# Other slots for the weight-combination steps, other places for three loads, and another order in the last batch, in a fused attention and two-layer MoE kernel

## The chip, the cores and the metric

One core of a Trainium2 chip runs the whole program in one launch. The metric is device time in microseconds (us). Engines are called as in the profile: PE (matmul), PEld (its weight loads), DVE (vector), ACT (scalar), POOL (GpSimd) and SP, the engine whose queue issues nearly every DMA here.

## What is computed

```python
# per batch of 8, per head: q, k, v are 576 x 64, p is 32 x 64
p_packed = softmax(scale * p @ k.T) @ v
x = softmax(scale * q @ p_packed.T) @ p_packed      # heads side by side: 4608 tokens x 512
h = x @ w_in;   g = h * cos(h);                 y = g @ w_out      # first MoE, 512 -> 2048 -> 512
h = y @ w_in2;  g = where(h >= 1, h, where(h <= -1, 0, (h + 1)**2 / 4));  out = g @ w_out2
```

## The kernel before

Activations are kept transposed, features on the partitions and tokens along the row. A batch is 576 tokens, two halves of 288 (`HB`), so nearly every elementwise instruction handles 128 x 576 elements and every large matmul has 288 columns. An fp32 product is made of three fp32r matmuls (`TERMS`): each operand is split into a high part (a rounding copy on ACT) and a low part (the difference, on DVE or POOL), and high x high, high x low and low x high are added up.

The program has four stages. Stage 1 does attention and the first up product (`up`, L503). Stage 2, `run_down1`, does the first down product with the cosine. Stages 3 and 4, `run_up2` and `run_down2`, are the second MoE, and the change lies in them. There the 2 x 2 block product is done with seven products instead of eight; they are called X1, Z6, Y5, X2, Z7, Y3 and Z4. The first letter names the accumulator in PSUM (`psX`, `psY`, `psZ`; two banks of Z, one of X and of Y): X1, Y5 and Z6 start it, the others are added to what stands there. So between two products on one accumulator somebody has to read the first result out: X1 is copied to `p1` by ACT, Z6 + p1 becomes `u` on DVE, Y5 + p1 becomes `q` on DVE; the sums `hh` are the four block results.

The seven products need combined inputs and combined weights.

- Combined weights (`su` of the up product, `sd` of the down product) are made by `combine` (L425), a generator with 13 steps for one unit of 2 x 128 rows: two loads; a scaling on ACT (L137); five conversion steps on DVE over 128 x 1024 elements (L144, L146, L150, L152, L156; the weights arrive as 64-bit numbers); two steps of small sums (L454, L455, L457, L458); then the highs on ACT (L444), the lows on DVE (L447) and the stores. Of the 16 units the last six, all of `sd`, are left for stage 3; the others are done before.
- Combined inputs of the up product come from `make_y` (L546): one load of a batch's y (1152 KB, `yb<-yT`), then eleven steps. Seven make a tile `ty` (the high on ACT, L75, the low on POOL, L76), four are differences on POOL (L558). In stage 3 this is all that POOL does.
- Combined inputs of the down product come from `source` (L849) on DVE and ACT, out of tiles `g` that `load_g` (L845) loads: four quarters b of four tiles each per batch.

Stage 3 runs over 8 batches p, 4 groups f of each and 7 products k of a group in the order X1, Z4 (of the group before), Z6, Y5, X2, Z7, Y3. One product is 12 matmuls, and what is written behind it is called a slot here; a batch has 28 slots, number 28p + 7f/2 + k. Behind product k comes `beside(k)` (L616): DVE sums (L597), the piecewise activation as two ACT instructions (L621, L625) and one on DVE (L629, "select"), and a store of the result `gT`. Nothing reorders this: the text of the program is the order on every engine, since `in_order` chains each engine's instructions as they are written. Two tables place the other work. A slot takes one step of `combine` if its number within the batch is in `UNIT_AT`, from slot `UNIT_FROM` on. `Y_AT` says how many steps of `make_y` for the next batch follow slot (f, k); two more steps follow slots (0, 0) and (0, 2) of the next batch. In the last batch a table `D2_AT` places the first loads of stage 4.

```python
    UNIT_AT = (20, 25, 27, 0, 1, 3, 6, 7, 8, 10, 13, 14, 15)
    Y_AT = {(2, 2): 3, (2, 6): 2, (6, 2): 1, (6, 4): 2, (6, 6): 1}
    ...
    D2_AT[0, 2] = d2_g0
    D2_AT[4, 3] = d2_g1
```

So one unit stretches from slot 20 of a batch to slot 15 of the next, and its heavy DVE steps stand at slots 27, 0, 1, 3 and 6.

Stage 4 goes through (batch, product, quarter c of the depth), each step 12 matmuls, 48 for a product, in the order `ORDER_DN`; the Z4 of a batch comes after X1 of the next one, only the last batch has it at the very end, straight after Z7. In the first steps g = 0, 1, 2, ... the loads stand by hand: at g = 1 quarter 2 of g, at g = 2 the weights of Z6 (2 x 1 MB), at g = 3 quarter 3. SP issues in this order, and its queue lands in this order.

Of the kernel before, what the change touches and what calls it, by code (L numbers as in the profile page):

```python
# [14 lines left out]
ALU = mybir.AluOpType  # L15
# [4 lines left out]
WO_FROM = 36  # L20
N_FIRST = 2
UNITS_1 = 8
UNIT_FROM = 20
FIRST_AT = (0, 5, 10, 13, 14)
SU_AT = tuple(range(70, 94, 4)) + (122, 124, 126, 127)
Y_LOAD = 112
# [3 lines left out]
PI = 3.141592653589793  # L30
TERMS = ((0, 0), (0, 1), (1, 0))
ORDER_UP = ("X1", "Z6", "Y5", "X2", "Z7", "Y3", "Z4")
ORDER_DN = ("X1", "Y5", "X2", "Z6", "Y3", "Z7", "Z4")


@with_exitstack
def body(ctx: ExitStack, tc: tile.TileContext, q, k, v, p, w_in, w_out, w_in2, w_out2, out):
    nc = tc.nc
    B, HP, _, S = q.shape
# [4 lines left out]
    HB = S // 2  # L44
# [46 lines left out]
    def begin_stores(keep=0):  # L91
        while len(stores) > keep:
            dst, src = stores.popleft()
            nc.sync.dma_start(out=dst, in_=src)
# [429 lines left out]
    SW, TY = {}, {}  # L524
# [62 lines left out]
    def wtile(pool, tag, bufs):  # L587
        return pool.tile([128, 2, HB], F32, tag=tag, name=tag, bufs=bufs)
# [197 lines left out]
        up2["rest"] = ys, eng, order[n_su[0]:]  # L786
        pd.close()

    UNIT_AT = (20, 25, 27, 0, 1, 3, 6, 7, 8, 10, 13, 14, 15)
    Y_AT = {(2, 2): 3, (2, 6): 2, (6, 2): 1, (6, 4): 2, (6, 6): 1}  # L790

    def run_up2():
        up2[5] = ctx.enter_context(tc.tile_pool(name="up_5", bufs=1, reuse_waits="tile", side="right"))
        for i in (8, 7, 6):
            up2[i] = pu.enter_context(tc.tile_pool(name=f"up_{i}", bufs=1, reuse_waits="tile", side="right"))
        up2["o"] = ctx.enter_context(tc.tile_pool(name="up_o", bufs=1, reuse_waits="tile"))
        ys, eng, rest = up2.pop("rest")
        old, n_fill = None, [0]
        eng[0] = nc.gpsimd
        for p in range(B):  # L800
            for f in range(0, 8, 2):
                at = {}
                cur = {"at": (p, f)}

                def fill(k):
                    x = 28 * p + f // 2 * 7 + k
                    if x >= UNIT_FROM and x % 28 in UNIT_AT:
                        step("wt")
                    if p == B - 1 and f == 6 and n_r[0] < 4 and k in (1, 3, 5, 6):
                        ahead()  # L810

                for k, o in enumerate(("X1", "Z4", "Z6", "Y5", "X2", "Z7", "Y3")):
                    if k != 1:
                        products_up(p, f, o, cur)
                    elif old:
                        products_up(*old["at"], o, old)
                    if p == f == 0 and k < 4:
                        if rest:
                            load_su(*rest.pop(0)), load_su(*rest.pop(0))
                        if k < 2:  # L820
                            next(ys, None)
                            next(ys, None)
                    beside(k, cur, old, fill)
                    begin_stores(1)
                    if (f, k) in ((0, 0), (0, 2)) and p:
                        next(ys, None)
                    if p + 1 < B:
                        if (f, k) == (0, 3):
                            ys = make_y(p + 1, eng)
                            next(ys)  # L830
                        for _ in range(Y_AT.get((f, k), 0)):
                            next(ys)
                    elif (f, k) in D2_AT:
                        D2_AT[f, k]()
                old = cur
        return old
# [8 lines left out]
    def load_g(p, b, c):  # L845
        t = GB[p, b, c] = GR[(4 * p + b) % 5][c]
        nc.sync.dma_start(out=t, in_=gT[b // 2 * 4 + c, :, 2 * p + b % 2])
# [31 lines left out]
    R = {}  # L879
    d2_seq = []  # L880
    for p_ in range(B):
        for o_ in ORDER_DN[:6]:
            d2_seq.append((p_, o_))
            if o_ == "X1" and p_:
                d2_seq.append((p_ - 1, "Z4"))
# [17 lines left out]
            load_g(0, 1, c)  # L903

    D2_AT[0, 2] = d2_g0
    D2_AT[4, 3] = d2_g1
    D2_AT[4, 0] = lambda: load_sd("X1")
    D2_AT[4, 2] = lambda: load_sd("Y5")
    D2_AT[4, 4] = lambda: load_sd("X2")
# [1 line left out]
    def run_down2(old):  # L911
# [26 lines left out]
        for g, (p, o, c) in enumerate(d2_seq):  # L938
# [3 lines left out]
            x, first = o[0], o in ("X1", "Y5", "Z6")  # L942
            if first and c == 0:
                s[x] = bank(x)
            ps, r = s[x], R.pop((p, o, c))
            for k in range(2):
                f = 2 * c + k
                w_ = SW[o, f // 4]
                for j in range(2):
                    for n, (w, y) in enumerate(TERMS):  # L950
                        nc.tensor.matmul(  # L951
                            out=ps[:, j], lhsT=w_[:, f % 4, w, j * 128:j * 128 + 128], rhs=r[:, y, k],
                            start=first and f == n == 0, stop=f == 7 and n == 2, skip_group_check=True,
                        )
            if g == 0:
                beside(0, None, old, none)
                products_up(*old["at"], "Z4", old)
# [6 lines left out]
            elif g < 5:  # L964
                beside(g + 1, None, old, none)
            begin_stores()
            if g in (1, 3):
                for i in range(4):
                    load_g(0, (g + 3) // 2, i)
            elif g == 2:  # L970
                load_sd("Z6")
            elif g in (5, 9, 12):
                load_sd(ORDER_DN[{5: 4, 9: 5, 12: 6}[g]])
# [2 lines left out]
                    source(*d2_todo.popleft())  # L976
            else:
                finish_source()
        finish(*d2_seq[-1][:2])
        begin_stores()  # L980

    E = mybir.EngineType
    items = [(n, hf, fp) for n, c in FIRST for hf in range(2) for fp in (2 * c, 2 * c + 1)]
# [278 lines left out]
```

## Time and profile before

| what | us |
|---|---|
| median of 3 runs | 1506.61 (1501.76 to 1513.17) |
| the profiled execution's own time | 1511.39 |
| its span on the chip | 1509.6 |
| PE busy in the span | 1470.4 |

Times of rows count from the start of the span. Stage 3 runs from 774.07 to 1142, stage 4 from 1142 to the end. "idle" and the brackets [us <-releaser] tell how long an engine stood idle before an instruction and what ended that.

### The profile page before, as it was taken

The page shows a single profiled execution, that of the slowest core. Times are in us where ns is not written, and L with a number is a line of the kernel's source. Part 1 is how long each engine was busy: PE and PEld are TensorE (multiplying, and loading weights), DVE is VectorE, ACT ScalarE, POOL GpSimd, SP SyncE. Part 2 cuts the span into 40 slices and gives each one's busy share as a digit, 9 for nine tenths or more (in the row PEclk, how much of TensorE's full clock was granted, in tenths as well). Part 3 has the DMA queues.
Part 4 walks back from the last instruction along what each step waited for, and adds up shares of the span by engine and source line. Part 5 has one row for each costly group of instructions (what it writes and reads, how often), then busy time and mean ns, then how long its engine had stood idle before and what let it go on. Part 6 is the DMA issues. An engine that isn't in the chain of part 4 may idle for free.

```text
span 1509.6 us, 29648 instructions
## 1 busy us (share of the span) xinstructions
PE 1470.4 (97%) x11796; PEld 1400.0 (93%) x11796; DVE 1173.9 (78%) x1682; ACT 907.8 (60%) x1424; POOL 139.8 (9%) x85
## 2 busy tenths in 40 slices
PE   8899999998999999999999999999999999999998
PEld 5678777788999999999999999999999999999998
DVE  7784676776888888888856889888867777777876
ACT  4455566667676667666647777777765444444442
POOL 0000000000000000000005335445310000000000
PEclk9899999999999999999999999999999999999999
DMA  9676777577555655766573664564568744344350
GB/s 352 204 236 226 254 272 270 199 238 254 166 162 171 197 186 187 270 219 187 177 286 133 213 210 162 176 218 172 190 240 339 267 153 128 114 134 142 119 157 33
DMA packets 156043, 302.36 MB, mean 200 GB/s; under 512 B 13568, under 2 KB 59648, under 8 KB 152320
## 3 DMA queue, kind: packets, MB, share of 16 engines
q1 hardware_dynamic: 155904, 300.47, 59.1%
q8 instruction: 92, 1.51, 0.4%
q14 instruction: 47, 0.39, 0.1%
HBM read 176.69 MB, written 123.73 MB: 199 GB/s over the span
## 4 chain that ended last, share of the span: by engine, by line
PE 82%; DVE 7%; DMA 7%; issue 2%; ACT 2%; SPq 0%; DVEq 0%; ACTq 0%
PE psZ L747 14%; PE psZ L951 10%; PE hps L512 9%; PE psZ L609 8%; PE psX L747 7%; PE psY L747 7%; PE psY L951 6%; PE psX L951 6%; PE psY L609 5%; PE psX L609 5%; DMA h1T<-u 3%; PE psS L275 2%; PE psM L218 2%; DVE t L629 1%; DMA yb<-yT 1%
## 5 line engine op out<-in xcount | busy, mean ns | idle before, releaser
L512 PEld LDWEIGHTS hps<-at,m 128*128 128x128 f32 x1536 | 209.4, 190 | 49.1 <-ACT u L518 19.9
L512 PE MATMUL hps<-at,m 128*128 128x288 f32 x1536 | 227.2, 303 | 10.4 <-ACT u L518 4.3
L747 PE MATMUL psZ<-r,wo 128*128 128x288 f32 x1536 | 206.1, 295 | 0.0
L747 PEld LDWEIGHTS psZ<-r,wo 128*128 128x128 f32 x1536 | 205.2, 188 | 0.0
L76 POOL TENSOR_TENSOR ty<-yb,ty 128x576 fp32r<-128x576 f32 x51 | 91.0, 1790 | 960.9 <-ACT ty L75 960.5
L857 ACT ACTIVATE r<-g 128x576 fp32r<-128x576 f32 x147 | 96.8, 681 | 125.5 <-DVE g L854 116.8
L715 ACT ACTIVATE r<-t 128x576 fp32r<-128x576 f32 x128 | 87.7, 685 | 129.0 <-PE psY L747 62.1
L720 DVE TENSOR_TENSOR r<-t,r 128x576 fp32r<-128x576 f32 x128 | 97.0, 757 | 57.8 <-ACT r L715 57.6
L518 ACT ACTIVATE u<-hps 128x576 f32<-128x576 f32 x128 | 83.0, 650 | 95.3 <-PE hps L512 58.1
L621 ACT ACTIVATE t<-hh,half 128x576 f32<-128x576 f32 x128 | 98.9, 772 | 50.9 <-DVE hh L597 45.1
L747 PE MATMUL psX<-r,wo 128*128 128x288 f32 x768 | 123.3, 296 | 1.7 <-ACT u L518 1.7
L747 PE MATMUL psY<-r,wo 128*128 128x288 f32 x768 | 123.2, 296 | 0.0
L629 DVE SCALAR_TENSOR_TENSOR t<-hh,t 128x576 f32<-128x576 f32 x128 | 114.0, 910 | 4.8 <-ACT t L625 4.8
L867 DVE TENSOR_TENSOR r<-g,r 128x576 fp32r<-128x576 f32 x147 | 107.4, 752 | 7.1 <-ACT r L857 7.1
L747 PEld LDWEIGHTS psX<-r,wo 128*128 128x128 f32 x768 | 109.4, 188 | 1.9 <-ACT u L518 1.9
L747 PEld LDWEIGHTS psY<-r,wo 128*128 128x128 f32 x768 | 109.4, 188 | 0.0
L951 PE MATMUL psZ<-r,so 128*128 128x288 f32 x768 | 104.6, 295 | 0.9 <-DVE hh L597 0.9
L951 PE MATMUL psY<-r,sw 128*128 128x288 f32 x768 | 104.9, 295 | 0.0
L951 PEld LDWEIGHTS psZ<-r,so 128*128 128x128 f32 x768 | 102.8, 188 | 1.1 <-ACT r L857 1.1
L951 PEld LDWEIGHTS psY<-r,sw 128*128 128x128 f32 x768 | 102.9, 188 | 0.3
L710 DVE TENSOR_TENSOR t<-h,t 128x576 f32<-128x576 f32 x128 | 96.2, 751 | 2.1 <-ACT t L705 2.1
L705 ACT ACTIVATE t<-t,halfpi 128x576 f32<-128x576 f32 x128 | 97.6, 762 | 0.0
(162 smaller groups left out, 2675.7 us busy)
## 6 DMA issues: line engine op xcount, KB each, us to landing
h1T<-u SPq DMA_DIRECT2D x128, 288.0 KB, 3.8
h<-h1T SPq DMA_DIRECT2D x128, 288.0 KB, 3.9
gT<-t SPq DMA_DIRECT2D x128, 288.0 KB, 2.9
g<-gT SPq DMA_DIRECT2D x85, 288.0 KB, 3.6
raw<-in_moe_w_out SPq DMA_DIRECT2D x32, 512.0 KB, 5.2
raw<-in_moe_w_in SPq DMA_DIRECT2D x28, 512.0 KB, 6.3
t<-gT SPq DMA_DIRECT2D x36, 288.0 KB, 4.3
k<-in_k SPq DMA_DIRECT2D x8, 1152.0 KB, 9.2
```

Of the source, the lines that this page charges most:

```text
L76: (eng or nc.gpsimd).tensor_tensor(out=lo, in0=src, in1=hi.bitcast(F32), op=ALU.subtract)
L512: nc.tensor.matmul(out=hps[:, j, :HB], lhsT=m[:, w, G, cs], rhs=x[:, G, y], start=(G == 0 and i == 0), stop=(G == 1 and i == 2),)
L609: nc.tensor.matmul(out=ps[:, i], lhsT=s[:, d, w, cs], rhs=t[:, d, y], start=first and d == n == 0, stop=d == 1 and n == 2, skip_group_chec ...
L621: nc.scalar.activation(out=t, in_=st["h", o], func=AF.Relu, scale=0.5, bias=half)
L629: nc.vector.scalar_tensor_tensor(out=t, in0=st["h", o], scalar=1.0, in1=t, op0=ALU.max, op1=ALU.min)
L705: nc.scalar.activation(out=t, in_=t, func=AF.Sin, scale=2 * PI, bias=halfpi)
L710: nc.vector.tensor_tensor(out=t, in0=G1.pop(i), in1=t, op=ALU.mult)
L720: nc.vector.tensor_tensor(out=r[:, 1], in0=turns.pop(i), in1=r[:, 0].bitcast(F32), op=ALU.subtract)
L747: nc.tensor.matmul(out=acc[d // 2][:, d % 2], lhsT=wo[f // 4, w][:, f % 4, ds], rhs=r[:, y, k], start=f == n == 0, stop=f == NFT - 1 and n ...
L857: nc.scalar.activation(out=r[:, 0], in_=b[out], func=AF.Copy)
L867: nc.vector.tensor_tensor(out=r[:, 1], in0=src, in1=r[:, 0].bitcast(F32), op=ALU.subtract)
L951: nc.tensor.matmul(out=ps[:, j], lhsT=w_[:, f % 4, w, j * 128:j * 128 + 128], rhs=r[:, y, k], start=first and f == n == 0, stop=f == 7 and ...
```

## The change

Five edits.

1. Steps of `combine` in stage 3 stand at other slots: the first unit starts at slot 33 (slot 5 of batch 1) instead of 20, and a unit stretches from slot 5 to slot 27 of one batch. No step is added or removed.
2. `make_y`'s steps: in every batch the pair of slot (2, 6) moves to (2, 4). In batch 0 the steps of group f = 2 move to f = 4, fourteen slots on.
3. Stage 4's first loads: quarter 1 of g (`d2_g1`) is issued at (2, 0) of the last batch instead of (4, 3), and quarter 3 at g = 2, before the weights of Z6, which go to g = 3.
4. The last batch of stage 4 has the order X1, Y5, Z6, X2, Z7, Y3, Z4.
5. The last product, Z4 of the last batch, is done one output half after the other: 24 matmuls, sum and store of 128 x 288, and again.

```diff
-UNIT_FROM = 20
+UNIT_FROM = 33
+ORDER_END = ("X1", "Y5", "Z6", "X2", "Z7", "Y3", "Z4")
...
-    UNIT_AT = (20, 25, 27, 0, 1, 3, 6, 7, 8, 10, 13, 14, 15)
-    Y_AT = {(2, 2): 3, (2, 6): 2, (6, 2): 1, (6, 4): 2, (6, 6): 1}
+    UNIT_AT = (5, 11, 13, 14, 15, 17, 19, 20, 21, 22, 24, 26, 27)
+    Y_AT = {(2, 2): 3, (2, 4): 2, (6, 2): 1, (6, 4): 2, (6, 6): 1}
...
-                        for _ in range(Y_AT.get((f, k), 0)):
+                        for _ in range(Y_AT.get((f - 2 * (p == 0 and f < 6), k), 0)):
...
-        for o_ in ORDER_DN[:6]:
+        for o_ in (ORDER_DN if p_ < B - 1 else ORDER_END)[:6]:
...
-    D2_AT[4, 3] = d2_g1
+    D2_AT[2, 0] = d2_g1
...
-            if g in (1, 3):
+            if g in (1, 2):
                 for i in range(4):
-                    load_g(0, (g + 3) // 2, i)
-            elif g == 2:
+                    load_g(0, g + 1, i)
+            elif g == 3:
                 load_sd("Z6")
...
-        finish(*d2_seq[-1][:2])
-        begin_stores()
+        y = wtile(pool, "hh", 3)
+        for j in range(2):
+            for c in range(4):
+                products(c, (j,))
+            nc.vector.tensor_tensor(out=y[:, j], in0=ps[:, j], in1=s["p1"][:, j], op=ALU.add)
+            nc.sync.dma_start(out=out[256 + j * 128:384 + j * 128, p * S:p * S + HB], in_=y[:, j])
```

In the step loop of stage 4 the matmuls of the last product are skipped and done at the end by a new inner function `products(c, js)`, which holds the same matmul loop as before with the output halves to do as an argument. Line numbers after the change are one higher up to L786.

The first place is ACT in batch 0 of stage 3, from the copy of X1's accumulator in group f = 2 on (`p_` is `p1`, L75 or L76 with `ty<-yb` the high part of a tile of batch 1). Before:

```order
L592 ACTIVATE p_9080<-psX 128x576
L621 ACTIVATE t<-hh,half 128x576
L625 ACTIVATE t<-t 128x576
L75 ACTIVATE ty<-yb 128x2x288
L621 ACTIVATE t<-hh,half 128x576
L625 ACTIVATE t<-t 128x576
L592 ACTIVATE hh<-psX 128x576
```

After the change, from the same copy:

```order
L593 ACTIVATE p_9080<-psX 128x576
L622 ACTIVATE t<-hh,half 128x576
L626 ACTIVATE t<-t 128x576
L622 ACTIVATE t<-hh,half 128x576
L626 ACTIVATE t<-t 128x576
L593 ACTIVATE hh<-psX 128x576
```

The high part of X1's tile no longer stands ahead of the copy `hh<-psX` that frees X's accumulator; it comes in the next group, f = 4, behind its `p1` copy and one activation pair.

The second place is DVE at the end of batch 1 and the start of batch 2 in stage 3 (`hh<-psZ,q` is the sum that reads Z7, `u<-psZ,p` the one that Z7 of the new batch waits for). Before:

```order
L597 TENSOR_TENSOR u<-psZ,p_9877 128x576
L597 TENSOR_TENSOR q<-psY,p_9877 128x576
L629 SCALAR_TENSOR_TENSOR t<-hh,t 128x576 x2
L597 TENSOR_TENSOR hh<-psZ,q 128x576
L144 TENSOR_SCALAR pa<-raw 128x1024
L597 TENSOR_TENSOR hh<-psY,u 128x576
L146 SCALAR_TENSOR_TENSOR pa<-raw,pa 128x1024
L629 SCALAR_TENSOR_TENSOR t<-hh,t 128x576
L150 TENSOR_SCALAR raw<-pa 128x1024
L597 TENSOR_TENSOR hh<-psZ,p_9877 128x576
L629 SCALAR_TENSOR_TENSOR t<-hh,t 128x576
L597 TENSOR_TENSOR u<-psZ,p_10014 128x576
```

After the change, the same stretch:

```order
L598 TENSOR_TENSOR u<-psZ,p_9858 128x576
L448 TENSOR_TENSOR raw<-raw,pl 128x512
L598 TENSOR_TENSOR q<-psY,p_9858 128x576
L630 SCALAR_TENSOR_TENSOR t<-hh,t 128x576 x2
L448 TENSOR_TENSOR raw<-raw,pl 128x512
L598 TENSOR_TENSOR hh<-psZ,q 128x576
L598 TENSOR_TENSOR hh<-psY,u 128x576
L630 SCALAR_TENSOR_TENSOR t<-hh,t 128x576
L598 TENSOR_TENSOR hh<-psZ,p_9858 128x576
L630 SCALAR_TENSOR_TENSOR t<-hh,t 128x576
L598 TENSOR_TENSOR u<-psZ,p_10006 128x576
```

The three conversion steps have left the batch's start (they stand in the same sequence at the start of group f = 4 now), and two lows (L448) stand ahead of the sum that reads Z7.

The third place is SP at the start of stage 4. Before:

```order
L847 DMA g<-gT 128x576 x4
L531 DMA sw<-sd 128x2048 x2
L94 DMA gT<-t 128x576
L847 DMA g<-gT 128x576 x2
L847 DMA t<-gT 128x576 x2
L94 DMA gT<-t 128x576
L531 DMA sw<-sd 128x2048 x2
```

After the change:

```order
L848 DMA g<-gT 128x576 x6
L848 DMA t<-gT 128x576 x2
L95 DMA gT<-t 128x576
L532 DMA sw<-sd 128x2048 x2
L95 DMA gT<-t 128x576
L532 DMA sw<-sd 128x2048 x2
```

Quarter 3 (the second four loads of g) now stands ahead of the 2 MB of Z6's weights.

## Rows read from the trace of the kernel before

**Rows 1.** Page, part 1: engine, busy us (share of the span), instructions.

```profile
PE 1470.4 (97%) x11796; PEld 1400.0 (93%) x11796; DVE 1173.9 (78%) x1682; ACT 907.8 (60%) x1424; POOL 139.8 (9%) x85
```

**Rows 2.** Waits of PE from 700 us on: total us, times, longest.

```profile
PE psZ L609 <- DVE u L597: 3.7, 6, 0.7
PE psX L951 <- DVE r L867: 2.8, 1, 2.8
PE psX L609 <- ACT hh L592: 2.0, 1, 2.0
PE psZ L951 <- DVE hh L597: 0.9, 1, 0.9
```

**Rows 3.** Timeline, batch 0 of stage 3: start, us, engine, line, tiles, [idle <-releaser].

```profile
793.24 1.76 PE L609 MATMUL psY<-ty,sw 128*128 128x288 f32 x12
794.37 0.68 ACT L75 ACTIVATE ty<-yb 128x576 fp32r<-128x576 f32 x1 [6.87 <-DMA yb<-yT]
...
797.02 2.60 PE L609 MATMUL psX<-ty,sw 128*128 128x288 f32 x12 [2.02 <-ACT hh L592]
...
803.43 1.75 PE L609 MATMUL psY<-ty,sw 128*128 128x288 f32 x12
```

**Rows 4.** Windows after that stall; the third number from the end is PEclk.

```profile
799.20:801.20 2.00, 2.00 (x10) 2.00 (x10) 0.09 (x1) 1.97 (x5) 2.00 (x2) 0.50 0.44 160
```

**Rows 5.** Timeline of PE: Z7 in batches 1 and 6, X1 of batch 7, stage 4's first.

```profile
829.79 1.89 PE L609 MATMUL psZ<-ty,sw 128*128 128x288 f32 x12 [0.60 <-DVE u L597]
...
1060.07 1.88 PE L609 MATMUL psZ<-ty,sw 128*128 128x288 f32 x12 [0.63 <-DVE u L597]
...
1097.35 1.75 PE L609 MATMUL psX<-ty,sm 128*128 128x288 f32 x12
...
1142.12 1.76 PE L951 MATMUL psX<-r,sm 128*128 128x288 f32 x12
```

**Rows 6.** Timelines of DVE, POOL and PE where batch 1 ends and 2 begins.

```profile
863.12 2.65 DVE L629 SCALAR_TENSOR_TENSOR t<-hh,t 128x576 f32<-128x576 f32 x2
865.69 0.74 DVE L597 TENSOR_TENSOR hh<-psZ,q 128x576 f32<-128x576 f32 x1
...
871.84 1.93 DVE L150 TENSOR_SCALAR raw<-pa 128x1024 int32<-128x1024 int32 x1
...
871.52 1.70 POOL L76 TENSOR_TENSOR ty<-yb,ty 128x576 fp32r<-128x576 f32 x1 [0.21 <-ACT ty L75]
...
868.63 1.78 PE L609 MATMUL psZ<-ty,so 128*128 128x288 f32 x12
```

**Rows 7.** Lines by form (busy, mean ns): first 420:770, without POOL; then 780:1130.

```profile
L150 DVE TENSOR_SCALAR raw<-pa 128x1024 int32<-128x1024 int32 x7 | 4.8, 690 | 0.0
...
L629 DVE SCALAR_TENSOR_TENSOR t<-hh,t 128x576 f32<-128x576 f32 x120 | 108.1, 920 | 4.8 <-ACT t L625 4.8
L447 DVE TENSOR_TENSOR raw<-raw,pl 128x512 fp32r<-128x512 f32 x12 | 15.0, 1254 | 0.0
L150 DVE TENSOR_SCALAR raw<-pa 128x1024 int32<-128x1024 int32 x6 | 11.5, 1922 | 0.0
```

**Rows 8.** Timeline, start of stage 4.

```profile
1140.70 0.76 DVE L597 TENSOR_TENSOR hh<-psZ,q 128x576 f32<-128x576 f32 x1 [0.44 <-PE psZ L609]
...
1142.67 0.78 ACT L621 ACTIVATE t<-hh,half 128x576 f32<-128x576 f32 x1 [2.92 <-DMA gT<-t]
...
1163.15 0.76 DVE L854 TENSOR_TENSOR g<-g,g 128x576 f32<-128x576 f32 x1 [5.43 <-DMA g<-gT]
...
1183.86 2.27 DVE L867 TENSOR_TENSOR r<-t,r 128x576 fp32r<-128x576 f32 x3 [3.28 <-ACT r L857]
1185.33 6.54 PE L951 MATMUL psX<-r,sm 128*128 128x288 f32 x48
```

**Rows 9.** Timeline, the last product, Z4 of the last batch, and the last sum.

```profile
1498.72 6.60 PE L951 MATMUL psZ<-r,so 128*128 128x288 f32 x48 [0.94 <-DVE hh L597]
1505.36 0.76 DVE L597 TENSOR_TENSOR hh<-psZ,p 128x576 f32<-128x576 f32 x1 [6.12 <-PE psZ L951]
```

More of the change, by code (lines that the diff above doesn't have):

```diff
@@ L944, in run_down2, with products @@
                 s[x] = bank(x)
[L945 to L954, printed above, removed]
+            ps = s[x]
+            last = (p, o) == (B - 1, "Z4")
+            def products(c, js):
+                r, first_k = R[p, o, c], first and c == 0
+                for k in range(2):
+                    w_ = SW[o, (2 * c + k) // 4]
+                    for j in js:
+                        for n, (w, y) in enumerate(TERMS):
+                            nc.tensor.matmul(
+                                out=ps[:, j], lhsT=w_[:, (2 * c + k) % 4, w, j * 128:j * 128 + 128], rhs=r[:, y, k],
+                                start=first_k and k == n == 0, stop=c == 3 and k == 1 and n == 2,
+                                skip_group_check=True,
+                            )
+            if not last:
+                products(c, range(2))
             if g == 0:
```

## The prediction

> **What bounds the kernel now.** I read the page's busy shares first, then the waits of PE for the stretch that the change touches, then the timelines around each wait. PE is busy 1470.4 of 1509.6 us [rows 1], so only its idle time can be won, and an edit that ends none of it is worth nothing. From 700 us on, where all five edits lie, PE waits in four ways [rows 2]: six times for the sum `u` on DVE, once for a low part of a source, once for a copy of X's accumulator on ACT, once for the sum before the very last product. That is 9.4 us; with the slow matmuls behind some waits, and the tail, it is about 17. This is the ceiling, 1.1% of 1506.61. A measurement of this kernel can tell about 1% from no change.
>
> The length of a slot is read from batch 7 of stage 3, in which nothing waits: 1097.35 to 1142.12 is 44.77 us for 28 products [rows 5], 1.60 us for one.
>
> **Batch 0 (edit 2).** ACT stands at L75, the first high of batch 1's y, for 6.87 us until the load `yb<-yT` has landed, at 794.37 [rows 3]. Behind it in ACT's order is the copy that frees X's accumulator, and PE waits 2.02 us for that. What it costs is read between two products: from the start of Y3 at 793.24 to the start of Y5 at 803.43 PE does four products, 10.19 us instead of 4 x 1.60 = 6.40. So 3.8 us, of which 2.0 is the wait; the rest is slow matmuls, and the granted clock behind the wait is 0.50 [rows 4], the lower level of 1.2 GHz. The change moves L75 from group 2 to group 4, 14 slots or 22.4 us on. ACT reached it at 794.37 - 6.87 = 787.5, so it will reach it near 809.9, 15 us after the landing. Nothing takes the wait's place there: POOL's five steps of batch 0 have the whole of group 4, and their tiles are first read in batch 1. I take all of it, **3.8**.
>
> **The batch boundaries (edit 1).** Z7 starts late in batches 1 to 6, each time released by `u` [rows 2, 5]. From batch 1 to batch 6 the distance is (1060.07 - 829.79) / 5 = 46.06 us a batch, against 44.77 in the quiet one: 1.29 too much, six times, 7.7 us. The idle alone is 0.6; the rest is again slow matmuls and small delays.
>
> Why `u` is late: ahead of it DVE does conversion steps, and they meet POOL. L150 takes 690 ns in stage 2, where POOL does nothing, and 1922 ns in stage 3 [rows 7]; the one at 871.84 ends 0.55 us after POOL's instruction of 871.52 to 873.22 [rows 6]. So it is not its own work but 1.24 us of standing still, more than the 0.6 that `u` lacks. After the change the same sequence (L144, L146, L150 between the sums, in the same slots of a group) stands at the turn from group 2 to group 4. POOL has five steps there in a row, at (2, 2) and (2, 4), which at 1.7 us each [rows 6] end about when the first conversion step is done, and then none until (6, 2). L150 should find POOL idle. So this wait goes, in all six batches.
>
> What comes late next is the other end of the unit. Its four lows (L447) stand in group 6 now, among POOL's remaining steps, and two of them ahead of the sum that reads Z7's accumulator, which Z4 of the next batch waits for. Before, that sum ran from 865.69 to 866.43 and Z4 began at 868.63 [rows 6]: 2.20 us to spare. The last low stands directly ahead of it. At the 1.25 us that lows took in stage 3 [rows 7] it leaves 0.95; blocked as L150 was, 1.93, it leaves 0.27. The low two places earlier takes another 1.25 at most, if no idle time of DVE takes it in: 1.93 + 1.25 - 2.20 makes a stall of 1.0. So the new wait lies between 0 and 1.0 a batch. I take 0.2, near the lower end, because DVE has no conversion step left behind the boundary and because `q`, between the two lows, waits for PE anyway. Six times 1.29 - 0.2: **6.5**, with bounds 1.7 and 7.7.
>
> A rule speaks against this edit. The Trainium skill, page "SBUF — State Buffer", section "Who interferes with whom", says that VectorE and GpSimd share a pair of ports as a lock: a VectorE instruction with two SBUF inputs, or in a two-port mode, and a GpSimd instruction shut each other out for a whole instruction, whoever comes first. By it each low may lose a full POOL instruction, the sum goes to the lower bound, and the whole would be 9.0 instead of 13.8; the trace's L150, whose end follows POOL's end, agrees with the rule.
>
> The scaling, the highs and the loads of a unit move as well. They lie on ACT and SP with slack: 6 slots (9.6 us) from the load to the scaling, 5 before; ACT is busy 60% [rows 1]. Nothing for them. A unit now ends at slot 27 of batch 6, 14 slots of batch 7 ahead of the first load of `sd`.
>
> **The start of stage 4 (edit 3).** PE waits 2.79 us in X2 for a low part on DVE [rows 2]. DVE stood idle 5.43 us until 1163.15 for a tile of g, for the difference of Z6 [rows 8]; the low of X2 was behind it in order. That tile is of quarter 3, issued behind 2 MB of Z6's weights in the same queue. With quarter 3 ahead of these weights it lands several us earlier, and the wait goes: 2.8. The weights come later by four loads of 288 KB, and Z6 needs them no earlier than X2's end.
>
> But the queue stays full and carries the same bytes. The next to be read is the first tile of batch 1: its low starts at 1183.86, behind ACT and the landing, takes some 0.75 and X1 starts at 1185.33 [rows 8], 0.7 to spare. With X1 due 2.8 earlier it lacks 2.1, unless the stream starts earlier. It does by some: the four loads of quarter 1 leave this stretch. The activation at 1142.67 waited 2.92 us for a store in that queue, while its input was ready at 1141.46 [rows 8], so up to 1.2 us on the way to the loads' issue goes too. Given back: 2.1 - 1.2 = 0.9. I take **1.9**, with bounds 0.7 (stream not earlier) and 2.8 (no give-back).
>
> **The last batch (edits 4 and 5).** The wait of 0.94 us before the last Z4 [rows 9] is there because Z7 and Z4 follow each other on one accumulator. Y3, 48 matmuls or 4 x 1.60 = 6.4 us, stands between them now and hides a sum of 0.76. The pairs that come to be neighbours by it (Y5 and Z6, X2 and Z7) have different accumulators. **0.9**.
>
> Behind the last matmul come a sum of 0.76 and, from 1506.12 to the span's end at 1509.6, 3.5 us of store and end. Half the columns make the sum some 0.3 shorter. The store of half the bytes saves between nothing and 1.7 (half of 3.5); I take 0.4, near the lower end, since most of such a time is not bytes when the queue is empty. The first half's sum and store lie beside 24 matmuls, 3.2 us. **0.7**, bounds 0.3 and 2.0.
>
> **The sum.** 3.8 + 6.5 + 1.9 + 0.9 + 0.7 = 13.8 us. From the profiled execution's 1511.39 that is 1497.6. This execution was 4.8 above the median of the runs; the waits lie in an order fixed by the program, so I take the same 13.8 from the median: 1506.61 - 13.8 = 1492.8, 0.9% less. By the lower bounds it is 3.8 + 1.7 + 0.7 + 0.9 + 0.3 = 7.4 (1499.2), by the upper 17.2 (1489.4).
>
> **Rivals.**
> - All the waits go and little comes back: 3.8 + 7.7 + 2.4 + 0.9 + 1.1 = 15.9, 1490.7. For it: six conversion waits of one kind, each with more time freed than it lacked. Against it: it needs the lows to slip through POOL's steps each time, and the full queue at 1183 to have moved along. It is the only case beyond 1%.
> - The wait moves to the other end of the unit: DVE's sum of Z7 comes 1.0 us late for Z4 in each of six batches, the boundary is worth 1.7, the whole 9.0, 1497.6. For it: two lows, two selects and three POOL steps in the same six slots, and 2.65 us for a pair of selects there already [rows 6]. Against it: before, there were 2.20 us to spare. The page on SBUF named above stands behind this one.
> - Slower: at the same place the four instructions ahead of that sum, two selects and two lows, are all blocked, each by 1.24 us, 5.0 in all. The lows alone use 1.4 of the 2.20 to spare, at L150's 0.69 each, so Z4 stalls 5.0 - 0.8 = 4.2 a batch, 25.2 in six. Against it 3.8 + 7.7 + 1.9 + 0.9 + 0.7 = 15.0 are won: 10.2 slower, 1516.8. It decides from a stall of 2.5 a batch. Against it: in the row of selects only one of the two was blocked [rows 6], and POOL has only four steps in group 6.
>
> **How the numbers follow.** The forecast (11 to 15 us won) has 0.45, the clean case 0.30, the moved wait (4 to 11) 0.20, slower 0.05, about 0.03 of it past 1%. Faster by over 1% is the clean case, 0.30; slower by over 1% 0.03; the rest, 0.67, within 1%. The range runs from the clean case, with a few us for the spread of medians (the three runs lie 11 us apart), to the moved wait with the same: 1487 to 1503.
>
> **What would show it.** In the new profile: no wait of ACT at L75 in batch 0, and no matmuls at clock 0.50 there; batches of stage 3 some 44.8 to 45.0 us apart; L150 at 0.69 us; the waits of PE for `u` gone, and in their place, if any, waits of Z4 for `hh` once a batch; X2 of stage 4 without a gap, and X1 of batch 1 with one of about 1 us; no gap before the last Z4. It is wrong if batches are still 46 us apart, if L150 is still at 1.9, or if PE's idle time has only gone to other places.

## The result, and the profile after

| | median us | runs | from to |
|---|---|---|---|
| before | 1506.48 | 6 | 1501.76 to 1513.17 |
| after | 1493.05 | 6 | 1487.41 to 1495.13 |

The ratio is 0.9903, with a 95% interval of 0.9874 to 0.9933. That is 13.4 us less; forecast were 13.8 less, 1492.8, within 1487 to 1503. A gain of 1% lies inside the interval. The profiled execution took 1489.83 us, with a span of 1488.1.

I read the profile in the same order as the one of before. First the page's busy shares, which answer to [rows 1]:

```profile
PE 1459.3 (98%) x11796; PEld 1394.7 (94%) x11796; DVE 1164.9 (78%) x1683; ACT 908.3 (61%) x1424; POOL 134.0 (9%) x85
```

PE does the same 11796 matmuls. It is busy for 11.1 us less, 6.9 of them ahead of stage 3, where the program is the same and the granted clock was higher (the last section tells of it), and idle for 28.8 us instead of 39.2. Then the waits of PE from 700 us on (us in total, times, longest), which answer to [rows 2]:

```profile
PE psZ L955 <- DVE hh L991: 0.6, 1, 0.6
PE psX L955 <- DVE r L868: 0.4, 1, 0.4
```

All four kinds of [rows 2] are gone, 9.4 us in nine waits. Two are left, 1.0 us in all: one is the give-back that the prediction had at the first tile of batch 1, the other is new.

To see where the time came from, the span is cut at four starts of PE's timeline. In the trace of after:

```profile
766.20 1.79 PE L610 MATMUL psX<-ty,sm 128*128 128x288 f32 x12
809.37 1.76 PE L610 MATMUL psX<-ty,sm 128*128 128x288 f32 x12
1124.38 1.76 PE L955 MATMUL psX<-r,sm 128*128 128x288 f32 x12
1209.79 2.41 PE L955 MATMUL psX<-r,sm 128*128 128x288 f32 x17
```

These are X1 of batches 0 and 1 of stage 3, stage 4's first product, and X1 of stage 4's batch 2. The trace of before has stage 4's first product at 1142.12 [rows 5], and the others at:

```profile
774.07 1.79 PE L609 MATMUL psX<-ty,sm 128*128 128x288 f32 x12
820.99 1.76 PE L609 MATMUL psX<-ty,sm 128*128 128x288 f32 x12
1229.94 4.27 PE L951 MATMUL psX<-r,sm 128*128 128x288 f32 x31
```

With the last sum's start and the span's end that gives a ledger in the prediction's own terms:

| stretch | before us | after us | won | forecast |
|---|---|---|---|---|
| batch 0 of stage 3 | 46.92 | 43.17 | 3.75 | 3.8 |
| batches 1 to 7 | 321.13 | 315.01 | 6.1 | 6.5 |
| stage 4, up to X1 of batch 2 | 87.82 | 85.41 | 2.4 | 1.9 |
| from there to the last sum's start | 275.42 | 275.07 | 0.35 | 0.9 |
| from there to the end of the span | 4.24 | 3.24 | 1.0 | 0.7 |
| sum | 735.53 | 721.90 | 13.6 | 13.8 |

The two spans differ by 21.5 us. The other 7.9 lie ahead of stage 3, where the program is the same: it starts at 774.07 before and at 766.20 after. What is known of these is told at the end; they are no part of the change.

**What DVE's steps take now.** The lines of 780:1130 by form, after (instructions | busy us, mean ns | idle before):

```profile
L630 DVE SCALAR_TENSOR_TENSOR t<-hh,t 128x576 f32<-128x576 f32 x125 | 119.6, 976 | 0.0
...
L448 DVE TENSOR_TENSOR pa<-pa,raw 128x512 fp32r<-128x512 f32 x6 | 4.1, 682 | 0.0
L151 DVE TENSOR_SCALAR raw<-pa 128x1024 int32<-128x1024 int32 x6 | 4.1, 681 | 0.0
...
L448 DVE TENSOR_TENSOR pa<-pa,raw 128x256 fp32r<-128x256 f32 x6 | 2.5, 417 | 0.0
```

The two lines L448 are two of a unit's lows. In the trace of before they take:

```profile
L447 DVE TENSOR_TENSOR pa<-pa,raw 128x256 fp32r<-128x256 f32 x6 | 9.9, 1653 | 0.0
L447 DVE TENSOR_TENSOR pa<-pa,raw 128x512 fp32r<-128x512 f32 x6 | 7.6, 1267 | 0.0
```

The conversion step L151 (L150 before) falls from 1922 ns [rows 7] to 681, and the two lows fall by 1.24 and 0.59 us: over six of each 18.4 us. But the selects rise from 920 [rows 7] to 976 ns, over some 120 of them 6.7 us, and the first two conversion steps are blocked as before (1259 and 1792 ns on the mean in both traces; 687 and 1218 in stage 2). So DVE still stands still behind POOL; over a third of the time won has only moved to other instructions, most of which have room behind them.

**The turn of a batch.** The timeline of DVE and PE where batch 2 ends and batch 3 begins, which answers to [rows 6]:

```profile
893.90 0.68 DVE L448 TENSOR_TENSOR raw<-raw,pl 128x512 fp32r<-128x512 f32 x1
...
895.37 3.03 DVE L630 SCALAR_TENSOR_TENSOR t<-hh,t 128x576 f32<-128x576 f32 x2
898.33 1.92 DVE L448 TENSOR_TENSOR raw<-raw,pl 128x512 fp32r<-128x512 f32 x1
900.17 0.74 DVE L598 TENSOR_TENSOR hh<-psZ,q 128x576 f32<-128x576 f32 x1
...
900.97 1.88 PE L610 MATMUL psZ<-ty,so 128*128 128x288 f32 x12
```

The low ahead of the sum is blocked at full size, 1.92 us, and Z4 starts 0.06 us behind the sum's end: the spare 2.20 us are used up. This is the moved wait. Batches 1 to 7 last 44.81, 45.12, 45.08, 44.97, 44.85, 45.16 and 45.01 us. In run 9 below, where that low stands elsewhere, they last 44.81, 44.91, 44.88, 44.81, 44.66, 44.83 and 44.77. So the moved wait costs 0.16 to 0.33 us in each of batches 2 to 7, on the mean 0.22.

**The start of stage 4**, which answers to [rows 8]:

```profile
1138.71 6.54 PE L955 MATMUL psX<-r,sw 128*128 128x288 f32 x48
...
1163.67 2.96 ACT L858 ACTIVATE r<-t 128x576 fp32r<-128x576 f32 x4 [5.77 <-DMA t<-gT]
1164.41 0.40 PE L955 MATMUL psX<-r,sm 128*128 128x288 f32 x1
1165.20 6.51 PE L955 MATMUL psX<-r,sm 128*128 128x288 f32 x47 [0.40 <-DVE r L868]
```

X2, the first line, runs its 48 matmuls in 6.54 us without a gap. X1 of batch 1 starts with one matmul and then waits 0.40 us for DVE's low, because its tile of g landed late: ACT stood 5.77 us for it. At its start, 40.03 us behind stage 4's first product against 43.21 before, 3.2 us are won; at X1 of batch 2 it is 2.4, so 0.8 is given back here.

**The end**, which answers to [rows 9]:

```profile
1477.47 3.35 PE L955 MATMUL psZ<-r,so 128*128 128x288 f32 x24
1480.85 0.46 DVE L991 TENSOR_TENSOR hh<-psZ,p 128x288 f32<-128x288 f32 x1 [1.76 <-PE psZ L955]
1481.37 3.46 PE L955 MATMUL psZ<-r,so 128*128 128x288 f32 x24 [0.55 <-DVE hh L991]
1484.86 0.46 DVE L991 TENSOR_TENSOR hh<-psZ,p 128x288 f32<-128x288 f32 x1 [3.55 <-PE psZ L955]
```

The first half of Z4 starts without a wait. The second half does not run beside the first half's sum: it waits for it.

### The profile page after: what moved, and what is told of

It reads as the page before. It is cut to its first block, busy times and chain, and to the rows that moved or that the text cites. A ratio compares the mean times of both kernels' runs of the same rounds, so it can differ in the third digit from the quotient of the medians.

```text
span 1488.1 us, 29660 instructions
## 1 busy us (share of the span) xinstructions
PE 1459.3 (98%) x11796; PEld 1394.7 (94%) x11796; DVE 1164.9 (78%) x1683; ACT 908.3 (61%) x1424; POOL 134.0 (9%) x85
## 4 chain that ended last, share of the span: by engine, by line
PE 86%; DVE 5%; DMA 5%; ACT 2%; issue 1%; SPq 0%; ACTq 0%; DVEq 0%
PE psZ L748 14%; PE hps L513 10%; PE psZ L955 10%; PE psZ L610 9%; PE psX L748 7%; PE psY L748 7%; PE psX L955 7%; PE psY L955 6%; PE psX L610 6%; PE psY L610 6%; DMA h1T<-u 3%; PE psS L276 1%; PE psM L219 1%; DMA t<-gT 1%; PE psS L219 1%
## 5 line engine op out<-in xcount | busy, mean ns | idle before, releaser
L77 POOL TENSOR_TENSOR ty<-yb,ty 128x576 fp32r<-128x576 f32 x51 | 86.2, 1691 | 950.3 <-ACT ty L76 949.8
L630 DVE SCALAR_TENSOR_TENSOR t<-hh,t 128x576 f32<-128x576 f32 x128 | 121.8, 971 | 0.0
```

Source lines behind the costliest of these rows:

```text
L630: nc.vector.scalar_tensor_tensor(out=t, in0=st["h", o], scalar=1.0, in1=t, op0=ALU.max, op1=ALU.min)
```

## The experiments

The theory of the prediction is that the batches are long because DVE's instructions stand still while POOL's run, so that a sum which PE waits for comes late. Its rivals: that the unit's steps are late by their number and place in DVE's order alone; that the load order gives nothing; that the gain lies elsewhere. A single time of a kernel here has some 8 us of spread that comes from ahead of stage 3, so each run is judged by distances within its own trace; a batch is the distance between two starts of X1.

**1. e1_pool_later**: the kernel before, with POOL's first differences for y moved off the turn of the batch.

```diff
-if (f, k) in ((0, 0), (0, 2)) and p:
+if (f, k) in ((0, 3), (0, 4)) and p:
...
-if (f, k) == (0, 3):
+if (f, k) == (0, 5):
```

> The kernel before with one thing moved: the two POOL steps that follow slots (0,0) and (0,2) of a batch follow (0,3) and (0,4), and the next load of y follows (0,5) instead of (0,3). DVE's own work and its order are those of before. Blocking theory (Z7 waits for u because POOL shuts L150 and a select out): L150 falls from 1922 to about 690 ns, PE's six waits for u go, batches 1 to 6 of stage 3 fall from 46.06 to about 44.9 us, in all 6 to 7 us less in stage 3. Amount theory (too much conversion work ahead of u, wherever POOL stands): L150 may fall, but the waits for u stay near 0.6 and the batches near 46.0.

1516.03 us in one execution, 1508.34 for the kernel before beside it; from stage 3's start to the end 738.6 us, against 735.5 in before, 1.6 of the difference in batches 1 to 7. The conversion step takes 682 ns, and no wait for `u` is left. But batches are 46.2 to 46.6 us long, not 44.9. PE waits for other sums instead, and a pair of selects early in the batch takes 3.23 us:

```profile
PE psY L609 <- DVE q L597: 4.0, 6, 0.9
PE psZ L609 <- DVE hh L597: 2.0, 6, 0.3
```

```profile
876.54 3.23 DVE L629 SCALAR_TENSOR_TENSOR t<-hh,t 128x576 f32<-128x576 f32 x2
```

POOL's moved steps now meet the two selects behind slots 4 and 5 (3.23 us, 1.41 in before). Behind them the first two lows of the unit (3.07 us for two) and the next such pair of selects (3.20) are blocked for longer than in before (2.85 and 2.00). Neither expectation came: the waits for `u` went, and the batches stayed long. So the simple form of the theory falls: it is not one instruction's standing still that makes `u` late. DVE builds up a lateness from all the blocked instructions of a stretch, and it shows at whichever sum PE needs next.

**2. e2_pool_into**: after, with the moved pair of y's steps put back among DVE's conversion steps, at (4, 0).

```diff
-Y_AT = {(2, 2): 3, (2, 4): 2, (6, 2): 1, (6, 4): 2, (6, 6): 1}
+Y_AT = {(2, 2): 3, (4, 0): 2, (6, 2): 1, (6, 4): 2, (6, 6): 1}
+Y_0 = {(4, 2): 3, (4, 4): 2, (6, 2): 1, (6, 4): 2, (6, 6): 1}
...
-for _ in range(Y_AT.get((f - 2 * (p == 0 and f < 6), k), 0)):
+for _ in range((Y_AT if p else Y_0).get((f, k), 0)):
```

> The changed kernel with POOL's pair of steps of slot (2,4) moved on to (4,0) in batches 1 to 7, into the slots of the conversion steps; DVE's order is that of the changed kernel. Blocking theory: L151 or the selects beside it are shut out again, L151 from 681 to between 1.3 and 1.9 us; two such instructions cost 2.5 us against 1.56 us that u has to spare in group 4 (it ends at 883.31, Z7 starts at 884.87), less 0.57 that L147 gets back, so PE waits for u again, 0.2 to 0.8 us in each of six batches, which come to 45.2 to 45.9 us. Amount theory: nothing changes, no wait for u, batches at 45.0.

1506.80 us. Batches 2 to 6 last 46.35 to 46.5 us, longer than in before. DVE and PE in one of them, then PE's waits:

```profile
888.57 1.99 DVE L630 SCALAR_TENSOR_TENSOR t<-hh,t 128x576 f32<-128x576 f32 x1
890.48 1.93 DVE L151 TENSOR_SCALAR raw<-pa 128x1024 int32<-128x1024 int32 x1
...
909.42 1.91 DVE L448 TENSOR_TENSOR raw<-raw,pl 128x512 fp32r<-128x512 f32 x1
912.06 1.19 PE L610 MATMUL psZ<-ty,so 128*128 128x288 f32 x7 [1.09 <-DVE hh L598]
```

```profile
PE psZ L610 <- DVE hh L598: 6.8, 6, 1.2
```

The conversion step is blocked again, at 1.93 us, and so is the select ahead of it. Expected was a wait for `u` of 0.2 to 0.8 us soon behind them; that did not come. PE waits some 20 us later, for the sum at the turn of the batch, and longer: DVE has no idle time between slot 14 and the turn, so what is lost is carried there and comes on top of the blocked low. The place of POOL's pair alone decides about 1.4 us a batch.

**3. e3_units_only**: before, with edit 1 alone.

```diff
-UNIT_FROM = 20
+UNIT_FROM = 33
...
-UNIT_AT = (20, 25, 27, 0, 1, 3, 6, 7, 8, 10, 13, 14, 15)
+UNIT_AT = (5, 11, 13, 14, 15, 17, 19, 20, 21, 22, 24, 26, 27)
```

> The kernel before with edit 1 alone (UNIT_FROM and UNIT_AT of the changed kernel; make_y's steps, the loads and the last batch as before). The pair of POOL steps then stands at (2,6), beside L146, a select and L150 in group 4. If edit 2's move to (2,4) is needed for edit 1 to pay, L150 is blocked again and PE waits for u in group 4 or the batches stay above 45.4 us; if edit 1 pays alone, batches 1 to 6 are at 44.8 to 45.2 us. In both cases batch 0 stays at 46.9 us, PE's wait of 2.0 us there and 2.8 us in X2 of stage 4 stay.

1502.02 us. Batches 1 to 6 last 273.30 us in all, 3.06 less than before's 276.36; with edit 2 it is 269.99. PE's wait at the turn, and two of DVE's instructions at the start of group 4:

```profile
PE psZ L609 <- DVE hh L597: 3.7, 6, 0.7
```

```profile
881.33 1.74 DVE L146 SCALAR_TENSOR_TENSOR pa<-raw,pa 128x1024 int32<-128x1024 int32 x1
882.99 1.99 DVE L629 SCALAR_TENSOR_TENSOR t<-hh,t 128x576 f32<-128x576 f32 x1
```

The conversion step is free here too (682 ns), but the pair at (2, 6) blocks the select ahead of it (1.99 us; 0.75 in after). The step ahead of that is blocked in both (1.74 here, 1.79 in after). So edit 1 alone brings half, and moving two of POOL's steps by two slots brings the other half.

Batch 0 lasts 45.05 us here, where 46.9 were expected, though the shift of edit 2 is not in it: ACT still waits 6.50 us for y's load and PE 1.64 behind it. PE's rows, and a window behind that wait (the third number from the end is the granted clock):

```profile
789.83 1.85 PE L609 MATMUL psX<-ty,sw 128*128 128x288 f32 x12 [1.64 <-ACT hh L592]
791.52 3.38 PE L609 MATMUL psZ<-ty,sw 128*128 128x288 f32 x24
```

```profile
790.00:792.00 2.00, 2.00 (x16) 2.00 (x17) 2.00 (x4) 1.92 (x4) 1.92 (x2) 1.00 0.42 156
```

In the trace of before the same groups took 2.60 [rows 3] and 4.17 us behind a wait of 2.02, part of them at 1.2 GHz [rows 4]. Here they take 1.85 and 3.38, and the clock stays at 1.00. The batch is 1.87 us shorter, half of the term of batch 0, for 0.38 us less of wait; the other 1.5 us are the clock. Edit 1 is not the cause: run 5, with the units at their old slots, has a wait of 1.67 us, a clock of 1.00 and 45.07 us, and run 1 a wait of 1.79, a clock of 0.50 and 46.73.

**4. e4_no_shift0**: after, without the shift of batch 0.

```diff
-for _ in range(Y_AT.get((f - 2 * (p == 0 and f < 6), k), 0)):
+for _ in range(Y_AT.get((f, k), 0)):
```

> The changed kernel without the move of make_y's steps in batch 0 (they follow group 2 again). My reading: ACT waits some 6.9 us at L76 for yb, PE about 2.0 us for the copy hh behind it, clock 0.50 behind that, and batch 0 goes from 43.17 back to about 46.9 us; everything else as in the changed kernel. Rival: the wait was a chance of that execution, or the end of the units in batch 0 removed it; then batch 0 stays at 43.2 to 44.

1498.09 us. Batch 0 lasts 50.59 us, not the 46.9 expected: 7.4 more than after and 3.7 more than before; the others are as in after. ACT and PE:

```profile
786.46 0.69 ACT L76 ACTIVATE ty<-yb 128x576 fp32r<-128x576 f32 x1 [6.67 <-DMA yb<-yT]
790.61 0.68 ACT L76 ACTIVATE ty<-yb 128x576 fp32r<-128x576 f32 x1 [2.09 <-POOL yb L559]
...
791.88 3.25 PE L610 MATMUL psX<-ty,sw 128*128 128x288 f32 x12 [4.59 <-ACT hh L593]
```

With the pair at (2, 4) a second high stands ahead of the copy that frees X's accumulator, and ACT waits for POOL as well. The move of the pair, which wins at the boundaries, would lose here without the shift: the two halves of edit 2 belong together.

**5. e5_no_pool_reads**: the kernel before, with POOL reading nothing; it leaves out the lows and the differences of y.

```diff
-split(t[:, :, 0], t[:, :, 1], src, eng[0])
+if eng[0] is nc.gpsimd:
+    nc.scalar.activation(out=t[:, :, 0], in_=src, func=AF.Copy)
+    nc.gpsimd.memset(t[:, :, 1].bitcast(F32), 0.0)
+else:
+    split(t[:, :, 0], t[:, :, 1], src, eng[0])
...
-eng[0].tensor_tensor(out=out, in0=a, in1=b, op=ALU.subtract)
+if eng[0] is not nc.gpsimd:
+    eng[0].tensor_tensor(out=out, in0=a, in1=b, op=ALU.subtract)
```

> The kernel before, in which stage 3's work on POOL is left out: the low parts of y's tiles are set to zero by an instruction that reads nothing, and the differences of y are not formed. DVE's instructions and their order are those of before, in the same slots. Blocking theory: L150 at 690, L146 at about 1220, L447 at about 685 and L629 at about 750 ns, no wait of PE for a DVE sum in stage 3, batches 1 to 6 at 44.8 us instead of 46.06. Amount theory (the conversion steps are too much DVE work at that place in any case): the waits for u stay, batches above 45.5.

1495.44 us, 1505.55 for the kernel before beside it. DVE has the order of before; POOL's lows are memsets, which only write. The lines of 780:1130:

```profile
L634 DVE SCALAR_TENSOR_TENSOR t<-hh,t 128x576 f32<-128x576 f32 x123 | 90.0, 751 | 5.0 <-ACT t L630 5.0
L556 POOL MEMSET ty<- 128x576 f32 x47 | 26.9, 582 | 290.3 <-PE psX L614 231.3 <-PE psY L614 31.5 <-PE psZ L614 22.7
L447 DVE TENSOR_TENSOR raw<-raw,pl 128x512 fp32r<-128x512 f32 x12 | 8.2, 683 | 0.0
...
L150 DVE TENSOR_SCALAR raw<-pa 128x1024 int32<-128x1024 int32 x6 | 4.1, 692 | 0.0
```

Selects 751 ns instead of 920, lows 683 instead of 1254, the conversion step 692 instead of 1922, all as without POOL. No wait for DVE is left in stage 3, and batches 1 to 6 last 268.9 us, 44.8 each. With the same order of steps the rival of place alone is out: the batches are long because DVE stands still behind POOL. The Trainium skill, page "SBUF — State Buffer", section "Who interferes with whom", says that an instruction of VectorE with two SBUF inputs meets a GpSimd instruction that reads SBUF, not one that only writes it. The selects agree: 14 of them run beside a memset here for more than 0.3 us and take their 0.75 us. No low and no conversion step meets a memset, so for these run 5 shows only what they take without POOL's reads. The conversion step has one SBUF input and met POOL's reads too (1922 ns), so of the two cases that this section of the Trainium skill names it could only be the other, a mode that takes both ports; no run here shows the mode.

**6. e6_weights_first**: after, with the weights of Z6 ahead of quarter 3 again.

```diff
-if g in (1, 2):
+if g in (1, 3):
     for i in range(4):
-        load_g(0, g + 1, i)
-elif g == 3:
+        load_g(0, (g + 3) // 2, i)
+elif g == 2:
     load_sd("Z6")
```

> The changed kernel with quarter 3 of g behind Z6's weights again (g = 1: quarter 2, g = 2: weights, g = 3: quarter 3); quarter 1 stays early. My reading: the wait in X2 of stage 4 is back, somewhat shorter than the 2.8 us of before because the stream starts 1.6 us earlier (1.2 to 2.8), and X1 of batch 1 finds its data there and has no wait; from stage 4's start to X1 of batch 1 it is 41 to 43.3 us, against 40.03 in the changed kernel and 43.21 before. Rival (the early quarter 1 alone removed the wait): no wait in X2, 40 us.

1496.49 us. X2 waits again:

```profile
1151.01 1.73 PE L955 MATMUL psX<-r,sw 128*128 128x288 f32 x11 [1.66 <-DVE r L868]
```

X1 of batch 1 waits for nothing then. It starts at 41.75 us of stage 4 (40.03 after), X1 of batch 2 at 86.37 (85.41 after, 86.07 in run 8). So the order of the loads takes a wait of 1.66 us from X2 and gives back most at X1; its net is between 0.3 and 1.0.

**7. e7_quarter1_late**: after, with quarter 1 of g back in stage 4's beginning.

```diff
-D2_AT[2, 0] = d2_g1
+D2_AT[4, 3] = d2_g1
```

> The changed kernel with quarter 1 of g loaded at (4,3) of the last batch again; quarter 3 stays ahead of Z6's weights. My reading: the loads at the start of stage 4 are issued 1.2 to 1.7 us later, so the full queue brings batch 1's first tile that much later: X1 of batch 1 waits that much longer, 1.6 to 2.2 us, instead of 0.4, and it stands 41.2 to 41.8 us behind stage 4's start instead of 40.03; the wait in X2 stays away or is under 1 us. Rival (quarter 1's place does not matter): 40.0 us.

1494.62 us. The first tile of batch 1 lands later, and X1 waits 1.85 us for ACT and then 0.40 for DVE:

```profile
1167.41 0.40 PE L955 MATMUL psX<-r,sm 128*128 128x288 f32 x1 [1.85 <-ACT r L858]
1168.20 8.04 PE L955 MATMUL psX<-r,sm 128*128 128x288 f32 x47 [0.40 <-DVE r L868]
```

X1 of batch 1 starts at 42.25 us of stage 4 (41.2 to 41.8 expected), X1 of batch 2 at 89.16: 3.1 to 3.8 more than in after and run 8. Of these 1.5 are the 47 matmuls behind the waits, 8.04 us instead of 6.51, at a granted clock of 0.51 in 1169 to 1171. Even without them the earlier place of quarter 1 is worth more than the order of quarter 3.

**8. e8_after_again**: after, unchanged, to see what repeats.

> The changed kernel itself, beside the next one on the same chip: about 13.5 us (0.9%) below the kernel before, stage 3's batches and stage 4's steps as in its first profile within 0.1 us.

1494.65 us (6 runs, 1488.88 to 1498.36) against 1504.38 (11 runs): ratio 0.9930, interval 0.9905 to 0.9954. That is 9.7 us less, not 13.5. Four of these six executions of after have a mean granted clock of 0.990 or 0.991, against four of the eleven of before at 0.989 or 0.990. The means of the executions at 0.991 and less differ by 12.3 us between before and after, those at 0.993 and more by 13.8. Batches of stage 3 are the same within 0.03 us; X1 of batches 1 and 2 of stage 4 starts 0.65 us later than in the first trace, outside the 0.1 expected. From stage 3's start to the end it is 722.6 us, against 721.9.

**9. e9_three_more**: after, with what is left taken away. The last two steps of a unit go to slots 27 and 0; 12 matmuls of Y3 stand between the halves of the last product; the load of Z4's weights at the start of stage 4 comes two steps (24 matmuls) later.

```diff
-UNIT_AT = (5, 11, 13, 14, 15, 17, 19, 20, 21, 22, 24, 26, 27)
+UNIT_AT = (5, 11, 13, 14, 15, 17, 19, 20, 21, 22, 24, 27, 0)
...
-elif g in (5, 9, 12):
-    load_sd(ORDER_DN[{5: 4, 9: 5, 12: 6}[g]])
+elif g in (5, 9, 14):
+    load_sd(ORDER_DN[{5: 4, 9: 5, 14: 6}[g]])
...
 for c in range(4):
-    products(c, (j,))
+    products("Z4", c, (j,))
+if j == 0:
+    products("Y3", 3, range(2))
```

> The changed kernel with three more edits, each at a wait that it has left: the last low stands behind slot 27 instead of 26 (behind the sum that reads Z7) and the last stores at slot 0; the last quarter of Y3's products in the last batch is done between the two halves of Z4; the weights of Z4 are loaded at g = 14 instead of 12, behind batch 1's first tiles. My reading of what is left: batches 1 to 7 fall by 0.2 each to about 44.8 (1.4 in all), the wait of 0.55 between the halves goes with its slow matmul (0.75), the wait of X1 in batch 1 of stage 4 goes (0.75); 2.9 us in all, about 1490 where the changed kernel has 1493. Rival for the first: the low only moves the lateness on to the next sum (that of Y3 or u of the new batch), and batches stay at 45.0; then 1.5 us.

1492.18 us (5 runs, 1491.52 to 1494.46): ratio to before 0.9914, interval 0.9894 to 0.9934. By medians it is not told from after. Within its trace it is: from stage 3's start to the end 718.9 us, 3.0 less than after and 3.7 less than run 8, where 2.9 were expected, and from 700 us on PE's list of waits is empty. Batches 1 to 6 last 268.90 us, as in run 5. The end:

```profile
1481.24 3.44 PE L956 MATMUL psZ<-r,so 128*128 128x288 f32 x24
1484.53 1.76 PE L956 MATMUL psY<-r,sw 128*128 128x288 f32 x12
1486.13 3.35 PE L956 MATMUL psZ<-r,so 128*128 128x288 f32 x24
```

So after leaves some 3 us of its stages 3 and 4 to be had, and with these no wait of PE is left there.

## Why the prediction was right

**Batch 0, 3.8 forecast, 3.75 measured.** ACT's wait and the matmuls at 1.2 GHz are gone and nothing came in their place. But the size is in part luck. Four traces have batch 0 in its old order: before and run 1, 46.92 and 46.73 us, where the clock fell behind the wait, and runs 3 and 5, 45.05 and 45.07, where it did not. Against 43.17 the shift is worth some 3.7 us in the one case and 1.9 in the other; the prediction read its price from one trace, of the dearer kind. And run 4 shows 7.4, the shift's worth next to the pair at (2, 4), a price that the prediction did not look for.

**The boundaries, 6.5 forecast, 6.1 measured.** The conversion step is at 0.68 us, the waits for `u` are gone in all six batches, and the moved wait has the size that was taken, 0.22 us a batch against 0.2. Two steps of the reasoning were right in their result and too narrow in their cause. "So it is not its own work but 1.24 us of standing still, more than the 0.6 that `u` lacks" puts the lateness on one instruction; run 1 freed that instruction and the batches stayed at 46.2 to 46.6, because other instructions were blocked instead. And "L150 should find POOL idle" rested on the pair at (2, 4): with that pair at its old place (run 3) the step was free as well, a select ahead of it was not, and only half of the gain came. A blocked last low was to take 1.93 us of the 2.20 to spare and took 1.92. But the 0.2 came about in another way than was reckoned: the low two places earlier, which in that sum makes the stall, takes 0.68 us at 893.90 and is not blocked, while the two selects ahead of the sum take 3.03 us instead of 2.65 [rows 6], which was not counted. That the pick between 0 and 1.0 was so near is luck.

**What became of the rivals.** The moved wait of 1.0 us does exist, but for another place of POOL's pair: run 2 has it with 1.2 us and a loss of 1.4 a batch. Four fully blocked instructions in a row, the way to a slower kernel, are not in after: there the two selects take 3.03 us, where two free ones take 1.41, and the last low 1.92. The clean case, 15.9, did not come with this change. Run 9 comes to it: 735.5 - 718.9 = 16.6.

**Stage 4's start, 1.9 forecast, 2.4 measured.** X2's wait went, X1 of batch 1 gave back 0.8 (0.9 forecast). But the prediction put the 2.8 on the order of quarter 3 alone and quarter 1 in as a help for the give-back. Runs 6 and 7, one trace each, show the weights the other way round: the order is worth 0.3 to 1.0, the early quarter 1 from 1.6 to 3.8, the more where the clock falls behind the wait. The stretch as a whole, too, differs by execution: four traces with the old start (before, runs 1, 3 and 5) have 87.82, 89.47, 89.70 and 90.72 us, four with the new one (after, runs 2, 4 and 8) 85.41, 85.76, 86.08 and 86.07. By these means it is worth 3.6. So of the two traces compared, before was dear in batch 0 and cheap here; that the sum came out so near is partly luck.

**The last batch, 0.9 forecast, 0.35 measured.** This is the step that failed: "The first half's sum and store lie beside 24 matmuls". In the built program the second half's first matmul waits for that sum, though it writes the other half of psZ's tile: 0.55 us idle, some 0.7 with the slower first matmul behind it. What Y3 hides ahead of Z4 was right (0.35 + 0.7, about 1.1 us). Run 9 puts other matmuls in that place and the wait is gone. Whether two separate tiles would do the same was not tried.

**The tail, 0.7 forecast, 1.0 measured.** The sum of half the columns takes 0.46 us instead of 0.76, as taken; the store and the end take 2.8 instead of 3.5, 0.7 less where 0.4 were taken.

**From the trace to the median.** The same 13.8 were taken off the median although the traced execution lay above it. That held: the sum from stage 3 on is 13.6, the medians differ by 13.4, and the traced executions by 21.6, of which 7.9 are of another origin. The medians of run 8 differ by 9.7, so their agreement to 0.4 us is luck as well.

## What to carry to other kernels

Where VectorE and GpSimd run beside each other, count how many of VectorE's instructions meet one of GpSimd's between two places where it has idle time: the lateness adds up and shows at the next result that TensorE needs, which may be 20 us behind the place where it arose. Price a moved step by what it stands next to at its new place, on both engines, and try two edits apart and together, since here each half of an edit was worth something else without the other. Read the price of a wait from several executions: here the same wait cost 1.5 us more in some of them. After splitting a product in halves, look in the built program whether the halves wait for each other.

## What the runs showed of the hardware that was not expected

**The time ahead of stage 3 has two values.** The granted clock in the first 60 us is 0.82 to 0.84 in some executions and 0.97 in others, for the same instructions. The windows 0:60 of before and of after (the third number from the end is the clock):

```profile
0.00:60.00 60.00, 52.17 (x449) 36.96 (x450) 43.96 (x81) 26.03 (x47) 0.70 (x6) 0.83 0.81 286
```

```profile
0.00:60.00 60.00, 52.08 (x532) 38.36 (x536) 47.86 (x88) 29.82 (x54) 0.70 (x6) 0.97 0.87 303
```

In the same 60 us PE does 449 matmuls in the one and 532 in the other. Of the eleven traces of both kernels and the experiments, those at 0.82 to 0.84 (before and runs 1, 2, 6 and 9) start stage 3 at 771.8 to 775.6 us, those at 0.97 (after and runs 3, 4, 5, 7 and 8) at 764.5 to 767.3. That is 8 us on the average, and most of the spread of a kernel's runs. What sets it was not found.

**A blocked instruction can lose more than its own time.** The conversion step grows from 0.69 to 1.92 us, a low from 0.68 to 1.92, a select from 0.75 to 1.99: each by up to 1.24 us, where POOL's instruction takes 1.4 to 2.4. The loss is what is left of POOL's instruction, less 0.13. In the timelines of before and after a select that meets one ends 0.61 to 0.62 us behind the end of POOL's, wherever in it the select came (but for its last 0.1 us); a low of 128 x 512 or the conversion step ends 0.55 us behind it. Yet in run 5 the 14 selects that ran beside a POOL write (582 ns each) lost nothing.

**Whether the clock falls behind a wait differs between executions, and the length of the wait alone does not decide it.** In batch 0 waits of 2.02 and 1.79 us (before, run 1) were followed by a granted clock of 0.50, which is 1.2 GHz, and waits of 1.64 and 1.67 (runs 3 and 5) by 1.00, 2.4 GHz. In X2 of stage 4, where the program is the same in these four, the wait of 2.79 us in before was followed by 1.00, and those of 2.67, 2.76 and 3.20 in runs 1, 3 and 5 by 0.50. Windows behind the wait in X2, in before and in run 3:

```profile
1166.00:1168.00 2.00, 2.00 (x17) 2.00 (x16) 2.00 (x4) 0.74 (x2) 0.00 (x0) 1.00 1.02 430
```

```profile
1156.00:1158.00 2.00, 2.00 (x10) 2.00 (x10) 2.00 (x4) 1.14 (x2) 0.00 (x0) 0.50 1.05 442
```

A fall cost 1.5 us in each of these places and in run 7. It makes up most of what the terms of batch 0 and of stage 4's start differ by from trace to trace. What decides it was not found.
